# Block-sparse attention with a GELU feed-forward: the last batch's keys and queries are asked for in the middle of the fourth half's attention

## The chip, the core and the metric

The kernel runs on one core of a Trainium2 chip. The metric is the device time of one execution in microseconds (us), lower is better. The engines are PE (TensorE: matrix products), DVE (VectorE), ACT (ScalarE), POOL (GpSimd) and SP (SyncE); each works through its own list of instructions in order and waits on semaphores for the others. Transfers are asked for by an instruction on POOL or SP and are carried out by 16 DMA engines.

## What is computed

```python
# q, k, v: 4 batches x 8 heads x 768 tokens x 64, float32; blocks of 32 tokens, 24 blocks
scores = scale * np.matmul(q, k.transpose(0, 1, 3, 2))
mask = np.abs(blk_i - blk_j) <= window
mask = mask | (blk_i == 0) | (blk_j == 0) | (blk_i == n_blocks - 1) | (blk_j == n_blocks - 1)
for qb in range(n_blocks):
    for kb in sampled_blocks[qb]:                     # 3 sampled blocks per block of queries
        mask[qb*block:(qb+1)*block, kb*block:(kb+1)*block] = True
attn = softmax(np.where(mask, scores, -1e9))
x = (attn @ v), heads put side by side: 3072 tokens x 512
h = x @ w_in                                          # 512 -> 2048
out = (0.5 * h * (1 + erf(h / sqrt(2)))) @ w_out      # 2048 -> 512, float32
```

Every block of queries sees its neighbours, the first and the last block and three sampled blocks. The first and the last block of queries see everything ("dense" rounds).

## The kernel before

The 4 batches are worked in 8 **halves** (`units`), two to a batch: an even half has the quads 1, 2, 0 and the dense rounds, an odd half the quads 3, 4, 5 and sparse rounds alone. The outer loop runs over the halves n = 0 to 7. One turn of it does the first feed-forward product of half n (`ffn1_step`, 8 steps of PE products and a GELU on ACT), then the attention of half n + 1, with the second feed-forward product of half n (`ffn2_pieces`) filled in between. So the fourth half, `units[3]`, is the second half of batch 1; its attention runs in the turn n = 2, and its first feed-forward product opens the turn n = 3.

The order in an attention is written out by hand as a string of words, `PLANS[n + 1]`: `s` scores (PE), `m` maxima (DVE, into a tile `nm`), `e` exponentials (ACT, from `nm`), `t` transposes (DVE), `w` the product with the values (PE, into `av`), `d` the division (DVE, into `xh`), `o` transposes on PE and copies to `xT` (ACT), `f` some products of the second feed-forward, `S` the stores that are due (ACT copies to `os`, SP sends), `G` the table of GELU, and `x` with a name: a function handed in by the caller. An attention may end with the first two rounds of the half after the next batch's border ("ahead").

Keys and queries of a batch come in two steps. POOL asks for them by tokens into the tiles `qn` and `kn` (`load_by_token`, L126: 6 transfers of 128 KB each). Then SP turns them with a transposing transfer: `turn_queries` (L136, `qn` to `qT`) and `turn_keys` (L133, `kn` to `ptd`, in the next turn). Ahead of the loads POOL copies one element into `mark` (`hold_loads`, L172), so that nothing behind it on POOL starts before that element is written. On POOL's list the loads of a batch are followed by another such mark and by the copies of sampled blocks for the next half (`gather`, L316); DVE does most of these copies itself (L316 too), after those of the fixed blocks (L295, L308).

For the last batch (b = 3) both loads and the turning of queries are issued in the turn n = 3, after the first step of the feed-forward. There `hold_loads` takes an element of `xT` that ACT writes in the last output but one of the fourth half's attention. `nm` and `xh` are tiles of a pool with four buffers to a name, so the fifth maximum after one waits until all that read the first are done.

Of the kernel before, what the change touches and what calls it, by code (L numbers as in the profile page):

```python
# [20 lines left out]
def kernel(  # L21
# [12 lines left out]
    B, H, S, D = q.shape  # L34
# [42 lines left out]
    kn = const.tile([P, H, PI * D], BF16, name="kn")  # L77
    qn = const.tile([P, H, PI * D], BF16, name="qn")
# [22 lines left out]
    def sampled(i, r):  # L101
        c0 = GW * (i // 3) + 4 * BW + DW * (i % 3) + BW * r
        return gb[:, c0:c0 + BW]
# [9 lines left out]
    def keys(b):  # L113
        return kvs[b % 2][:, :, 0:KC]
# [5 lines left out]
    def by_token(x):  # L120
        return x.rearrange("p h c -> p (h c)")[:, 0:S * H * D // P]

    def load_by_token(dst, src, b):
        rows = by_token(dst).rearrange("p (c h d) -> p c h d", h=H, d=D)
        for c in range(NC):
            nc.gpsimd.dma_start(out=rows[:, c],  # L126
                                in_=src[b, :, P * c:P * c + P].rearrange("h p d -> p h d"))
# [7 lines left out]
    def turn_queries(b):  # L135
        nc.sync.dma_start_transpose(out=qTs[b % 2].rearrange("p c r s -> p (c r) s"), in_=by_token(qn))  # L136
# [33 lines left out]
    def hold_loads(x):  # L170

        nc.gpsimd.tensor_copy(mark, x)  # L172
# [146 lines left out]
    class Unit:  # L319
        def __init__(self, b, quads, dense):  # L320
# [10 lines left out]
            for grp in self.groups:  # L331
# [4 lines left out]
    units = [Unit(b, quads, dense) for b in range(B)  # L336
             for quads, dense in (((1, 2, 0), True), ((3, 4, 5), False))]
    groups_of = {rnd: grp for unit in units for grp in unit.ends.values() for rnd in grp}
    column = {}
    for n, unit in enumerate(units):  # L340
        for t, quad in enumerate(unit.quads):
            for i in range(4):
                column[unit.b, 4 * quad + i] = (xTs[n % 2], P * t + BL * i)

    st = {}

# [78 lines left out]
    def table(func):  # L425

        nc.scalar.activation(junk, zero[0:1, 0:1], func)  # L427
# [164 lines left out]
    def store_finished():  # L592
        while finished:
            store(*finished.pop(0))
# [17 lines left out]
    def attention(unit, filler, plan, extra={}, ahead=None):  # L612

        done = begun.pop(unit, 0)
        rounds = [(unit, rnd) for rnd in unit.rounds[done:]]
        if ahead:
            begun[ahead] = AHEAD
            rounds += [(ahead, rnd) for rnd in ahead.rounds[0:AHEAD]]  # L620
        groups = dict(zip("dabc" if unit.dense else "abc", [grp for _, grp in sorted(unit.ends.items())], strict=True))
        todo = {f"{k}{i}" for k in "smet" for i in range(len(rounds))}
        todo |= {k + c for k in "wdo" for c in groups}
        tall = False
        for word in plan.split():
            what, arg = word[0], word[1:]
            if what in "sfwoOx":

                before, tall = tall, what in "sw" and arg[0] != "d"
            if what == "s":  # L630
                at = [int(i) for i in arg.split("+")]
                scores(rounds[at[0]][0], *[rounds[i][1] for i in at])
                todo -= {f"s{i}" for i in at}
                continue
            if what == "f":
                for _ in range(int(arg)):
                    next(filler, None)
                continue
            if what == "x":
                extra[arg]()  # L640
                continue
            if what == "S":
                store_finished()
                continue
            if what == "G":
                table(AF.Gelu)
                continue
            if what in "met":
                {"m": maxima, "e": exponentials, "t": turned}[what](rounds[int(arg)][1])
            elif what == "w":  # L650
                halves = tuple(int(h) for h in arg[1:]) or (0, 1)
                values(unit, groups[arg[0]], halves, before)
                if 1 not in halves:
                    continue
                word = word[0:2]
            elif what == "d":
                divided(groups[arg])
            elif what in "oO":
                outputs(unit, groups[arg], 1 + (what == "O"))
            todo.remove(word.lower())  # L660
        assert not todo, todo
        for _ in filler:
            pass
        store_finished()
# [56 lines left out]
    def more_numbers(js):  # L721
        def load():
            for c in range(0, len(js), 6):
                known.update(block_numbers(js[c:c + 6], DVE))
        return load
# [14 lines left out]
    def next_keys(b):  # L740
# [3 lines left out]
    PLANS = {  # L744
# [20 lines left out]
    for n, unit in enumerate(units):  # L765
        nxt = units[n + 1] if n + 1 < len(units) else None
        b = unit.b
        fresh = nxt is not None and nxt.b != b
        if nxt is not None and not fresh:
            if n == 0:  # L770
                nc.vector.tensor_copy(kvs[0][:, :, 0:KC], k0)
                more_numbers(J1[3:8])()
            gather_fixed(keys(b), nxt.place)
            gather(nxt, J1[:8], known)
            if n == 0:
                more_numbers(J0[:3])()
        for s in range(KOUT // 2):
            ffn1_step(n, 2 * s)
            if s == 0:
                if n == 0:  # L780
                    hold_loads(sampled(nxt.place[J1[7]], NR - 1)[0:1, BW - 1:BW])
                    gather(nxt, J1[8:], others, engine=nc.gpsimd)
                    ones(1)
                elif fresh and b + 2 < B:
                    xT, t0 = column[b, unit.groups[-2][0]]
                    hold_loads(xT[0:1, 0, t0:t0 + 1])
                    load_by_token(qn, q, b + 2)
                    load_by_token(kn, k, b + 2)
                    turn_queries(b + 2)
                elif nxt is not None and not fresh:  # L790
                    if b + 1 < B:
                        turn_keys()
                        hold_loads(sampled(nxt.place[J1[7]], NR - 1)[0:1, BW - 1:BW])
                        load_values(b + 1)
                    else:
                        gather(nxt, J1[8:], others, engine=nc.gpsimd)
            if s == 7 and nxt is not None:
                table(AF.Exp)
                if n > 0 and not fresh and b + 1 < B:
                    next_keys(b + 1)  # L800
                    hold_loads(keys(b + 1)[0:1, NB, 0:1])
                    gather(nxt, J1[8:], others, engine=nc.gpsimd)
            if fresh and s == 0:
                gather_fixed(keys(b + 1), nxt.place)
                gather(nxt, J0[3:9], known)
                gather(nxt, J0[:3], known)
                hold_loads(sampled(nxt.place[J0[2]], NR - 1)[0:1, BW - 1:BW])
                gather(nxt, J0[9:], others, engine=nc.gpsimd)
        filler = ffn2_pieces(n)
        if nxt is None:  # L810
            last_output(n)
        elif n == 0:
            def later_values():
                hold_loads(qTs[1][0:1, 0, 1, 0:1])
                load_values(1)
            extra = {f"{w}{pr}{end}": partial(turn_pair, w, pr, end == "d")
                     for w in "kq" for pr in range(NPR) for end in ("", "d")}
            attention(nxt, filler, PLANS[1], extra | {"v": later_values, "s": partial(spare_key, keys(1))},
                      ahead=units[n + 2])
        else:  # L820
            attention(nxt, filler, PLANS[n + 1], ahead=units[n + 2] if not fresh and b + 1 < B else None)


# [28 lines left out]
```

## Time and profile before

| | |
|---|---|
| time, median of 3 runs (lowest to highest) | 273.91 us (272.92 to 274.8) |
| the profiled execution: time | 274.32 us |
| the profiled execution: span from first to last instruction | 272.5 us |
| PE, ACT, DVE, POOL busy | 93%, 76%, 75%, 38% of the span |
| packets of POOL's DMA queue (q0), of SP's (q1) | 57440 and 18418 |
| transfers from POOL for `qn` and `kn` by tokens | 12 each, 128 KB |

The profile has the time of one execution; the span leaves out what lies before the first and behind the last instruction. A page of the profile gives the busy time of each engine, then the span cut in slices, the DMA queues, the chain of work that ended last, and groups of instructions. The trace behind it can be asked for a timeline of one engine (start, length, engine, line, operation, tiles, and in brackets the idle time before it with what ended it), for the chain of waits in order of time, and for the DMA queues in a stretch of the span (packets, MB, and the time of the packets as a share of 16 engines, which passes 100% where packets overlap). In all views "issue" is time in which an engine waited for nothing that the profile shows.

### The profile page before, as it was taken

To read this page: it belongs to the slowest core of one execution; us is meant where nothing else is said; L and a number is where in the kernel's file an instruction comes from. 1 tells how busy PE (TensorE), PEld (TensorE's weight loads), DVE (VectorE), ACT (ScalarE), POOL (GpSimd) and SP (SyncE) were. 2 spreads that over 40 slices of the span, in tenths; PEclk is the share of its full clock that TensorE was granted. 3 is DMA by queue.
4 is the path that set the end of the run, shared out by engine and by line. 5 is a ranking of instruction groups with operands and counts; after the bars stand their busy time and mean duration, and the time that the engine had idled before them with its cause. 6 is when DMAs were issued, how large, how long until landed. Compare 5 with 4: busy or idle time off the path is not lost.

```text
span 272.5 us, 11555 instructions
## 1 busy us (share of the span) xinstructions
PE 252.6 (93%) x4944; PEld 144.1 (53%) x4944; DVE 203.3 (75%) x472; ACT 206.7 (76%) x381; POOL 103.6 (38%) x212
## 2 busy tenths in 40 slices
PE   0899679999999999999999799999999999999994
PEld 0634455455664656545554466455655655465543
DVE  7499659599897988699989686698869892981000
ACT  8789655977869975897779755995889956986611
POOL 7799960735964000940991002920040160000000
PEclk9999999999999999999999999999999999999999
DMA  6999399979999117921999017911101110021012
GB/s 96 186 191 149 55 147 202 206 123 143 93 172 129 43 41 158 104 28 68 98 156 172 8 41 156 117 43 44 38 1 43 43 41 0 5 79 41 0 38 82
DMA packets 75910, 24.41 MB, mean 90 GB/s; under 512 B 65489, under 2 KB 72914, under 8 KB 75858
## 3 DMA queue, kind: packets, MB, share of 16 engines
q0 software_dynamic: 57440, 13.64, 53.4%
q1 hardware_dynamic: 18418, 10.03, 15.5%
q8 instruction: 39, 0.64, 1.0%
q14 instruction: 13, 0.11, 0.1%
HBM read 27.26 MB, written 6.29 MB: 123 GB/s over the span
## 4 chain that ended last, share of the span: by engine, by line
PE 82%; ACT 7%; issue 3%; DMA 3%; DVE 3%; POOL 1%; POOLq 0%; ACTq 0%
PE hp L536 30%; PE op L579 26%; PE av L481 10%; PE sc L356 6%; DMA qn<-in_q_dram 3%; PE tx L513 2%; PE op L608 2%; ACT pp L399 2%; PE av L442 2%; PE pt L241 2%; ACT pp L403 2%; PE av L608 1%; DVE xh L501 1%; ACT L427 1%; ACT gb L295 1%
## 5 line engine op out<-in xcount | busy, mean ns | idle before, releaser
L536 PE MATMUL hp<-xT,w_in_sb 128*128 128x384 bf16 (+2 forms) x536 | 85.1, 319 | 1.4 <-issue 1.4
L579 PE MATMUL op<-w_out_sb,g 128*128 128x512 bf16 x336 | 83.4, 380 | 0.4 <-issue 0.4
L399 ACT ACTIVATE pp<-sc,nm 128x256 bf16<-128x256 f32 x176 | 74.2, 544 | 4.4 <-DVE nm L382 3.8
L536 PEld LDWEIGHTS <-w_in_sb 128*128 128x128 bf16 x536 | 51.2, 98 | 34.5 <-issue 1.5
L558 ACT ACTIVATE g<-hp 128x768 bf16<-128x768 f32 x56 | 45.1, 809 | 25.6 <-PE hp L536 25.6
L382 DVE TENSOR_REDUCE nm<-sc 128x4 f32<-128x1024 f32 (+1 forms) x48 | 53.0, 1119 | 12.3 <-PE sc L356 11.9
L579 PEld LDWEIGHTS <-g 128*128 128x128 bf16 x336 | 29.4, 98 | 33.9 <-issue 6.0
L316 DVE COPY gb<-kv 128x392 bf16 x177 | 35.8, 282 | 0.0
L416 DVE STREAM_TRANSPOSE pT<-pp 128x512 f32<-128x512 f32 (+1 forms) x48 | 30.6, 652 | 2.8 <-ACT pp L399 2.6
L172 POOL COPY mark<-gb 1x1 bf16<-1x1 bf16 x6 | 1.1, 179 | 80.9 <-DVE gb L316 80.9
L316 POOL COPY gb<-kv 128x392 bf16 x54 | 26.3, 537 | 14.1 <-PE av L481 13.8
L481 PEld LDWEIGHTS <-pT 64*32 64x32 bf16 (+1 forms) x2400 | 25.5, 91 | 7.3 <-issue 2.1
L481 PE MATMUL av<-kv,pT 64*32 64x130 bf16 (+1 forms) x1344 | 27.4, 221 | 1.7 <-issue 0.9
L521 ACT COPY xT<-tx 128x512 bf16<-128x512 bf16 (+3 forms) x34 | 13.7, 432 | 14.0 <-PE tx L513 14.0
L148 POOL DMA_DIRECT2D kv<-in_v_dram x32 | 23.0, 727 | 2.4 <-issue 2.4
L356 PE MATMUL sc<-gb,qT 64*32 64x256 bf16 x704 | 18.1, 273 | 2.2 <-issue 1.5
L356 PEld LDWEIGHTS <-qT 64*32 64x32 bf16 x832 | 9.9, 90 | 18.1 <-issue 10.0
L427 ACT ACT_TABLE_LOAD x15 | 19.2, 1283 | 0.3
L501 DVE TENSOR_TENSOR xh<-av,rec 128x512 bf16<-128x512 f32 (+2 forms) x28 | 18.2, 652 | 1.0
L385 DVE TENSOR_REDUCE nm<-sc 128x1 f32<-128x768 f32 x16 | 14.8, 949 | 4.6 <-PE sc L356 4.6
L403 ACT ACTIVATE pp<-sc,nm 128x768 bf16<-128x768 f32 x16 | 17.0, 1106 | 1.2 <-DVE nm L385 0.9
L481 PE MATMUL av<-gb,pT 64*32 64x130 bf16 x924 | 17.3, 222 | 0.5 <-issue 0.5
(80 smaller groups left out, 247.2 us busy)
## 6 DMA issues: line engine op xcount, KB each, us to landing
out_dram<-os SPq DMA_DIRECT2D x23, 256.0 KB, 2.1
kv<-in_v_dram POOLq DMA_DIRECT2D x32, 96.0 KB, 3.3
w_in_sb<-in_moe_w_in_dram POOLq DMA_DIRECT2D x4, 512.0 KB, 7.1
w_out_sb<-in_moe_w_out_dram POOLq DMA_DIRECT2D x2, 1024.0 KB, 13.5
kn<-in_k_dram POOLq DMA_DIRECT2D x4, 384.0 KB, 11.4
qn<-in_q_dram POOLq DMA_DIRECT2D x4, 384.0 KB, 12.7
qn<-in_q_dram POOLq DMA_DIRECT2D x12, 128.0 KB, 4.9
kn<-in_k_dram POOLq DMA_DIRECT2D x12, 128.0 KB, 5.3
```

The lines of the kernel that those rows point to most:

```text
L148: nc.gpsimd.dma_start(out=kvs[b % 2][32 * hh:32 * hh + 32, 0:NB, c0:c0 + D], in_=v[b, h].rearrange("(n p) d -> p n d", p=BL))
L316: (engine or nc.vector).tensor_copy(to[:, None, :], src[:, bass.ds(at[j][r], 1), :])
L356: nc.tensor.matmul(o, lhsT=qT[rows, j // 4, pr, BL * (j % 4):BL * (j % 4) + BL], rhs=rhs(rows, pr), start=True, stop=True)
L382: nc.vector.tensor_reduce(out=nm[:, 0:2 * n].rearrange("p (g j) -> p g j", g=2), in_=A4[:, :, 0:n, :], op=ALU.max, axis=AX.X, negate=True)
L399: nc.scalar.activation(at[:, x // n, x % n], A[:, a:a + 256].rearrange("p (e c k) -> p e c k", e=2, k=BL), AF.Exp, bias=nm[:, x:x + 1])
L403: nc.scalar.activation(pp[:, 0:S].rearrange("p (c k e) -> p c e k", e=2, k=BL), A[:, 0:S].rearrange("p (c e k) -> p c e k", e=2, k=BL), AF ...
L416: nc.vector.transpose(pt.rearrange("p g c x -> p (g c) x")[:, :, 64 * s:64 * (s + n)].bitcast(F32), pp[:, 0:512 * n].bitcast(F32).rearrang ...
L427: nc.scalar.activation(junk, zero[0:1, 0:1], func)
L481: nc.tensor.matmul(av[32 * s:32 * (s + w), h, VS * G:VS * G + V2], lhsT=pv[rows, G, c % 4, BL * s:BL * (s + w), c // 4], rhs=src[rows], st ...
L536: nc.tensor.matmul(hp[:, i, c0:c1], lhsT=w_in_sb[:, ki, (m + i) * P:(m + i + 1) * P], rhs=xTs[n % 2][:, ki, c0:c1], start=(ki == 0), stop= ...
L558: nc.scalar.activation(g[:, m:m + 2, 0:T], hp[:, :, 0:T], AF.Gelu)
L579: nc.tensor.matmul(op, lhsT=g[:, m, t * P:(t + 1) * P], rhs=w_out_sb[:, m, :], start=(m == 0), stop=(m == KOUT - 1))
```

## The change

The loads and the mark ahead of them become a function, `later_batch(b, x)`. For batch 2 it is called where the code stood. For batch 3 it is handed to the attention of the fourth half as the word `xl`, which stands in `PLANS[3]` behind `m2`; the mark there takes an element of the `nm` of round 2, written by that `m2`. The turning of the queries stays where it was.

```diff
+    def later_batch(b, x):
+        hold_loads(x)
+        load_by_token(qn, q, b)
+        load_by_token(kn, k, b)
...
-        3: ("f1 s3 s1 m3 s0 f5 m1 e3 f2 e1 f2 m0 t3 e0 f6 s2 m2 e2 f3 t1 f5 t0 f4 s4 m4 t2 wa s7 f1 m7 f2 e4 "
+        3: ("f1 s3 s1 m3 s0 f5 m1 e3 f2 e1 f2 m0 t3 e0 f6 s2 m2 xl e2 f3 t1 f5 t0 f4 s4 m4 t2 wa s7 f1 m7 f2 e4 "
             "f2 da f2 s5 m5 f1 t4 e7 f2 S e5 s6 m6 t5 wb S e6 oa f1 db t6 wc f1 ob dc f4 t7 oc G f1"),
...
                 elif fresh and b + 2 < B:
-                    xT, t0 = column[b, unit.groups[-2][0]]
-                    hold_loads(xT[0:1, 0, t0:t0 + 1])
-                    load_by_token(qn, q, b + 2)
-                    load_by_token(kn, k, b + 2)
+                    if b == 0:
+                        xT, t0 = column[b, unit.groups[-2][0]]
+                        later_batch(b + 2, xT[0:1, 0, t0:t0 + 1])
                     turn_queries(b + 2)
...
         else:
-            attention(nxt, filler, PLANS[n + 1], ahead=units[n + 2] if not fresh and b + 1 < B else None)
+            def batch_after():
+                later_batch(b + 2, st[nxt.rounds[2], "nm"][0:1, 0:1])
+            attention(nxt, filler, PLANS[n + 1], {"l": batch_after},
+                      ahead=units[n + 2] if not fresh and b + 1 < B else None)
```

The order of instructions is the same on every engine before and after. What differs is what POOL's mark reads, and the waits that follow from it. On POOL, around that mark (L172; `kv` and `gb` are the tiles that its copies of sampled blocks read and write; the names in brackets are the semaphores waited for: DMAHW of SP's transfers, DMASW of POOL's own):

```order
 L316 ISA
 L316 COPY gb<-kv_84 128x392 [waits PE_49]
-L172 COPY mark<-xT_92 1x1 [waits Activation_49,Pool_49]
+L172 CAST mark<-nm 1x1 [waits DVE_49,Pool_49]
 L126 DMA qn<-in_q_dram 128x8x64 [waits DMAHW2_49,DMASW2_49]
 L126 DMA qn<-in_q_dram 128x8x64 [waits DMASW3_49]
```

Only the mark's source has changed, and so the engine that releases POOL: DVE instead of ACT. On DVE, in the fourth half's attention, from the maximum that the mark now reads (`nm_3201`) to the one that takes its buffer again, before:

```order
L382 TENSOR_REDUCE nm_3201<-sc_3184 128x4 [waits PE_49]
L416 STREAM_TRANSPOSE pT_3215<-pp_3162 128x8x64 [waits Activation_49]
L416 STREAM_TRANSPOSE pT_3215<-pp_3173 128x8x64 [waits Activation_49]
L382 TENSOR_REDUCE nm_3244<-sc_3227 128x4 [waits DVE_49,PE_49]
...
L385 TENSOR_REDUCE nm_3362<-sc_3352 128x1 [waits DVE_49,PE_49]
...
L382 TENSOR_REDUCE nm_3394<-sc_3385 128x2 [waits PE_49]
...
L385 TENSOR_REDUCE nm_3415<-sc_3406 128x1 [waits PE_49]
```

and after:

```order
L387 TENSOR_REDUCE nm_3201<-sc_3184 128x4 [waits PE_49]
L421 STREAM_TRANSPOSE pT_3228<-pp_3162 128x8x64 [waits Activation_49]
L421 STREAM_TRANSPOSE pT_3228<-pp_3173 128x8x64 [waits Activation_49]
L387 TENSOR_REDUCE nm_3257<-sc_3240 128x4 [waits DVE_49,PE_49]
...
L390 TENSOR_REDUCE nm_3375<-sc_3365 128x1 [waits DVE_49,PE_49]
...
L387 TENSOR_REDUCE nm_3407<-sc_3398 128x2 [waits PE_49]
...
L390 TENSOR_REDUCE nm_3428<-sc_3419 128x1 [waits PE_49,Pool_49]
```

The last of these maxima now waits for POOL too, since POOL's mark reads the buffer that it takes.

## The prediction, made before the changed kernel was run

> **What bounds the kernel now.** I read the page first: busy times, then the chain that ended last.
>
> ```profile
> PE 252.6 (93%) x4944; PEld 144.1 (53%) x4944; DVE 203.3 (75%) x472; ACT 206.7 (76%) x381; POOL 103.6 (38%) x212
> ...
> q8 instruction: 39, 0.64, 1.0%
> ...
> PE 82%; ACT 7%; issue 3%; DMA 3%; DVE 3%; POOL 1%; POOLq 0%; ACTq 0%
> ```
>
> PE is the bound; what the other engines do matters only where it makes PE wait. The third row is a DMA queue of its own kind: 39 packets of "instruction", 0.64 MB. PE has 4944 products and 4944 weight loads, 253 instructions for each packet: I read these packets as PE's program arriving in pieces.
>
> So I went to the place that the change touches. POOL's timeline from 114 us on shows when the last batch's loads are issued now:
>
> ```profile
> 114.66 4.16 POOL L316 COPY gb<-kv 128x392 bf16 x9
> 129.36 0.30 POOL L172 COPY mark<-xT 1x1 bf16<-1x1 bf16 x1 [10.55 <-ACT xT L521]
> 129.89 6.06 POOL L126 DMA_DIRECT2D qn<-in_q_dram  x6 [0.23 <-issue]
> 135.94 5.34 POOL L126 DMA_DIRECT2D kn<-in_k_dram  x6
> ...
> 141.40 2.79 POOL L316 COPY gb<-kv 128x392 bf16 x6
> ```
>
> POOL stands idle for 10.55 us until ACT has written `xT`, then issues 12 transfers until 135.94 + 5.34 = 141.28. SP's timeline beside it:
>
> ```profile
> 121.56 10.98 SPq L565 DMA_DIRECT2D out_dram<-os  x3
> 140.29 5.48 SPq L136 DMA_TRANSPOSE qT<-qn  x1
> ```
>
> The turning of the queries starts at 140.29, when the queries have landed; the third store ahead of it is out by 121.56 + 10.98 = 132.54.
>
> Last I read the chain of waits there, for what PE lost:
>
> ```profile
> 130.55 10.40 PE hp L536 x64
> ...
> 148.65 1.25 PE av L442 x78
> 149.91 1.48 issue
> 151.38 0.47 PE av L442 x18
> ...
> 154.65 0.46 issue
> ...
> 207.49 1.49 PE av L442 x96
> ```
>
> The dense value product (L442, 96 matmuls) of the fifth half breaks off after 78 for 1.48 us with nothing to wait for. The last row is the same product of the seventh half, where no batch is loaded any more: 1.49 us in one piece. What the DMA queues did in the 4.1 us ahead of the pause, and then in the next 1.1 us:
>
> ```profile
> q1 hardware_dynamic: 1919, 0.52, 101.6%
> q0 software_dynamic: 986, 0.12, 46.9%
> ...
> q1 hardware_dynamic: 152, 0.22, 55.2%
> q8 instruction: 1, 0.02, 5.4%
> q0 software_dynamic: 8, 0.00, 1.0%
> ```
>
> From 144.8 to 148.9 us the DMA engines are full with the transposing transfer (q1) and the last keys (q0), and no piece of program comes. From 148.9 to 150.0 both run dry, one piece comes, and PE goes on at 151.38. So I take the pause for a piece of PE's program that stood behind that traffic. This is the only large loss of PE that the moved loads can touch.
>
> **The change part by part.** The order of instructions is the same on all engines; only the mark's source moves, and with it the time of the loads. DVE's timeline: copies of sampled blocks, the maximum that the mark now reads, the one that takes its buffer again, copies again, and the maximum behind them:
>
> ```profile
> 103.94 4.18 DVE L316 COPY gb<-kv 128x392 bf16 x24
> ...
> 117.53 1.23 DVE L382 TENSOR_REDUCE nm<-sc 128x4 f32<-128x1024 f32 x1
> ...
> 125.44 0.92 DVE L385 TENSOR_REDUCE nm<-sc 128x1 f32<-128x768 f32 x1
> ...
> 132.69 8.11 DVE L316 COPY gb<-kv 128x392 bf16 x27
> 141.58 1.23 DVE L382 TENSOR_REDUCE nm<-sc 128x4 f32<-128x1024 f32 x1 [0.77 <-PE sc L356]
> ```
>
> *When the loads run.* `nm` is written at 117.53 + 1.23 = 118.76, POOL's copies end at 114.66 + 4.16 = 118.82. So the mark runs at about 118.8 instead of 129.36, 10.5 us earlier, and the 12 issues fill about 119.3 to 130.5 (11.4 us before, 6.06 + 5.34). As the queries land well ahead of 132.5, SP's third store sets the turning: about 132.5 instead of 140.29. The landing times of the page:
>
> ```profile
> kn<-in_k_dram POOLq DMA_DIRECT2D x12, 128.0 KB, 5.3
> qT<-qn SPq DMA_TRANSPOSE x2, 10.8
> ptd<-kn SPq DMA_TRANSPOSE x2, 6.8
> ```
>
> The last keys land about 130.5 + 5.3 = 136, the turned queries at 132.5 + 6.8 to 10.8 = 139 to 143 (6.8 is the turning of keys, which has the queues more to itself). Both lie within PE's 10.40 us of the feed-forward, 130.55 to 140.95, or just behind it, and the queues are empty when the piece of program is due that came late at 148.9.
>
> *Gain: the pause at 149.91*, 1.48 us, goes whole: −1.48 (bounds −1.48 and 0). What hangs on that product, DVE's division and ACT's copies, moves up with it. *The pause at 154.65*, 0.46 us, comes with empty queues; it is a short block of quick products and I let it stay: 0 (bounds −0.46 and 0).
>
> *Cost: the same lateness in the fourth half's attention.* The loads now run where PE also takes program. Between 119 and 130 us, before:
>
> ```profile
> q1 hardware_dynamic: 288, 0.52, 12.8%
> q8 instruction: 2, 0.03, 1.1%
> ```
>
> Two pieces come in an almost empty DMA, and PE's chain has no issue pause there. After, q0 is full in that stretch. The nearest rows are in the second half's attention, PE's timeline, and the DMA queues from 63.4 to 65.9 us:
>
> ```profile
> 58.98 0.27 PE L481 MATMUL av<-kv,pT 64*32 64x130 bf16 x9 [0.27 <-issue]
> 67.26 1.02 PE L579 MATMUL op<-w_out_sb,g 128*128 128x512 bf16 x4 [0.36 <-issue]
> q0 software_dynamic: 2504, 0.31, 197.1%
> q8 instruction: 1, 0.02, 3.2%
> ```
>
> Here q0 was full with loads of values of the same kind (packets of about 125 bytes), and the pieces still came, with pauses of 0.27 and 0.36 us. From below the cost is 0, from above 1.48 for each of the two, the pause at 149.91. I take 0.27 + 0.36 = +0.63, since q0 alone made those, and 1.48 took the transposing transfer, which is not there then.
>
> *The mark* costs what it did (0.30 us): 0. *The new wait on DVE* stands at the maximum of 125.44; the mark is done by about 119.2, 6 us earlier: 0. Behind it on DVE stand the last transposes and divisions of that attention, for which PE's output transposes wait, so a late POOL would show; POOL's list ahead of the mark ends at 118.82, which covers it. *DVE beside POOL's issues:* its copies of sampled blocks took 8.11 / 27 = 0.30 us beside the issues and 4.18 / 24 = 0.17 us without. They would now end about 3.4 us earlier, near 137.3, and POOL's own six copies near 140 instead of 144.2. Neither is worth anything: PE's feed-forward lasts until 140.95, and DVE's next maximum already waits 0.77 us for PE. In the attention DVE now works beside the issues; what it does there:
>
> ```profile
> 61.68 0.70 DVE L416 STREAM_TRANSPOSE pT<-pp 128x512 f32<-128x512 f32 x1
> 121.71 0.70 DVE L416 STREAM_TRANSPOSE pT<-pp 128x512 f32<-128x512 f32 x1
> ```
>
> The first ran beside POOL's issues of values, the second with POOL idle, at the same 0.70: 0. *SP's queue:* stores and turning keep their order, and the three stores ahead of the turning wait for ACT alone, as before: 0.
>
> **Sum:** −1.48 + 0.63 = −0.85 us. The profiled execution took 274.32, so 273.5 against its own time; it lies 0.41 above the median, so 273.1 against the median of 273.91.
>
> **The rivals.**
> A, the forecast: the late piece comes in time and small pauses come instead; 273.91 − 1.48 − 0.46 + 0 = 272.0 at best to 273.91 − 1.48 + 1.48 = 273.9.
>
> B, nothing is gained: the pause isn't the traffic's doing but that of this place in the program, and it comes again, with or without the 0.63: 273.9 to 274.5. Against it speaks the seventh half's unbroken product, for it that one pause with one packet is a single case, and that the pause at 154.65 comes with empty queues. The Trainium skill, Runtime: NRT & Kernel Launch, section Instruction fetch mechanics, says that PE holds 2048 instructions and refills in blocks of 256, so that crossing a block is mostly hidden; by that rule a piece late by a few us would not stop PE, and the time would be B's. The trace agrees with the 256 (253 worked out above) but not with the depth: PE stopped around the very arrival of one piece.
>
> C, slower: the loads' packets hold up both pieces of program in the fourth half as the transposing transfer did at 148.9, 1.48 each: 2 × 1.48 − 1.48 = +1.48, so 275.4. It decides as soon as the two together lose more than the 1.48 gained. For it: there PE takes a piece every 3 to 4 us, not every 15 as in the feed-forward, and stores share the queues. Against it: 0.27 and 0.36 in the second half under a full q0.
>
> **How the numbers follow.** A 0.62, B 0.18, C 0.14, something else 0.06. The time is A's, 273.1. The range goes from 271.9 (both pauses gone, no new one) to 274.8 (B's upper end of 274.5, and some tenths for the spread of the runs); it holds A and B and leaves out C's upper part. About 1% (2.7 us) is what a measurement of this kernel can tell from no change: A, B and C all lie within it. For slower by over 1% C would have to double (0.05); for faster, as much would have to be found at a place that I don't see (0.03).
>
> **What would show each step.** POOL's mark at about 119 and the issues until 130.5; SP's turning near 132.5; no packet of q0 or q1 but stores after 143; the dense value product in one piece; DVE's 27 copies at some 4.7 us; in PE's waits, issue pauses of some tenths between 119 and 130. I am wrong in the gain if the pause at L442 stays though the queues are empty; in the cost if PE's issue pauses between 119 and 130 sum to over 1.5 us or to none; and altogether if DVE's maximum waits for POOL.

## The result, and the profile after

The changed kernel takes 276.85 us (median of 6 runs, 275.47 to 278.99) against 274.0 for the kernel before in the same series (272.92 to 274.8): 1.0124 times as long, 95% interval 1.0082 to 1.0167. It is slower, and the time lies above the stated range of 271.9 to 274.8. Ratios leave out executions more than 1.5% above the fastest of their kernel and medians don't, so for kernels that spread widely the two differ.

The profile after is of an execution of 277.17 us. The page, with the same lines as before:

```profile
span 275.4 us, 11555 instructions
PE 253.7 (92%) x4944; PEld 145.4 (53%) x4944; DVE 200.1 (73%) x472; ACT 206.1 (75%) x381; POOL 102.9 (37%) x212
```

The span grew by 2.9 us, PE's busy time by 1.1: PE waits more. Where, says the chain of waits around the change (start, length, what):

```profile
125.69 0.84 PE av L486 x84
126.53 0.59 issue
127.13 0.63 PE av L486 x20
...
130.73 0.14 PE tx L518
130.87 3.10 issue
133.97 0.29 PE tx L518 x3
134.25 0.86 PE op L584 x4
135.12 10.41 PE hp L541 x64
```

Two issue pauses stand in the fourth half's attention, where there was none: 0.59 and 3.10 us. The second cuts four small transposes after the first. The DMA queues from 126.3 to 131.3 us, and then to 132.5 us (packets, MB, share of 16 engines):

```profile
q0 software_dynamic: 5041, 0.64, 199.5%
q1 hardware_dynamic: 149, 0.27, 15.4%
...
q0 software_dynamic: 1391, 0.18, 230.8%
q8 instruction: 1, 0.02, 5.5%
```

In five microseconds 5041 packets of the loads pass and no piece of program; the next piece comes between 131.3 and 132.5 us, and PE goes on at 133.97. The fifth half, where the pause of 1.48 us stood before, on PE's timeline:

```profile
151.53 1.69 PE L584 MATMUL op<-w_out_sb,g 128*128 128x512 bf16 x7
153.15 1.56 PE L447 MATMUL av<-kv,ptd 64*64 64x130 bf16 x96
154.91 0.41 PE L361 MATMUL sc<-gb,qT 64*32 64x256 bf16 x16 [0.21 <-ACT pp L404]
```

The dense value product runs its 96 matmuls in one piece. So the gain came, and a larger cost of the same kind came in another place. To keep the two apart I use the length of an attention on PE, worked out from the trace: from the start of the last product of one first feed-forward to the start of the first product of the next one. Fourth half: 17.93 us before, 21.97 after, +4.04. Fifth half: 21.73 before, 20.18 after, −1.55. All other attentions behind the change agree within 0.1 us. The sum, +2.49, and 0.5 us that the profiled execution had lost ahead of the change (first feed-forward of the third half at 102.75 instead of 102.22) make the span's 2.9, with an end that is 0.2 us shorter.

POOL, SP and DVE after, each from its timeline:

```profile
119.43 0.18 POOL L172 CAST mark<-nm 1x1 bf16<-1x1 f32 x1
119.96 5.27 POOL L126 DMA_DIRECT2D qn<-in_q_dram  x6 [0.35 <-issue]
125.18 4.43 POOL L126 DMA_DIRECT2D kn<-in_k_dram  x5
129.90 0.88 POOL L126 DMA_DIRECT2D kn<-in_k_dram  x1 [0.29 <-DMA qn<-in_q_dram]
```

```profile
122.07 15.04 SPq L570 DMA_DIRECT2D out_dram<-os  x3
137.41 3.74 SPq L136 DMA_TRANSPOSE qT<-qn  x1
```

```profile
125.96 0.92 DVE L390 TENSOR_REDUCE nm<-sc 128x1 f32<-128x768 f32 x1
...
133.76 4.71 DVE L316 COPY gb<-kv 128x392 bf16 x27
```

POOL's mark and issues stand where they were forecast. DVE's maximum with the new wait has no idle time before it. The turning came at 137.41, since the third store ahead of it hangs on PE products behind the long pause (ACT copies them to `os` at 136.19).

### The profile page after: what moved, and what is told of

Read it like the earlier page. It is cut to its first block, busy times and chain, and to the rows that moved or that the text cites. A ratio compares the mean times of both kernels' runs of the same rounds, so it can differ in the third digit from the quotient of the medians.

```text
span 275.4 us, 11555 instructions
## 1 busy us (share of the span) xinstructions
PE 253.7 (92%) x4944; PEld 145.4 (53%) x4944; DVE 200.1 (73%) x472; ACT 206.1 (75%) x381; POOL 102.9 (37%) x212
## 4 chain that ended last, share of the span: by engine, by line
PE 79%; ACT 9%; issue 4%; DMA 3%; DVE 2%; POOL 1%; POOLq 0%; ACTq 0%
PE hp L541 30%; PE op L584 24%; PE av L486 10%; PE sc L361 5%; ACT pp L404 4%; DMA qn<-in_q_dram 3%; PE tx L518 2%; PE op L613 2%; ACT pp L408 2%; PE pt L241 2%; ACT L432 1%; PE av L613 1%; PE av L447 1%; DVE xh L506 1%; ACT gb L295 1%
## 5 line engine op out<-in xcount | busy, mean ns | idle before, releaser
L172 POOL COPY mark<-gb 1x1 bf16<-1x1 bf16 x6 | 1.1, 179 | 94.4 <-DVE gb L316 94.4
L316 DVE COPY gb<-kv 128x392 bf16 x177 | 32.8, 266 | 0.0
L486 PEld LDWEIGHTS <-pT 64*32 64x32 bf16 (+1 forms) x2400 | 26.7, 94 | 7.1 <-issue 1.9
L486 PE MATMUL av<-kv,pT 64*32 64x130 bf16 (+1 forms) x1344 | 28.5, 227 | 0.8 <-DVE pT L421 0.7
L486 PE MATMUL av<-gb,pT 64*32 64x130 bf16 x924 | 17.5, 223 | 0.7 <-issue 0.6
```

The costliest lines, as they stand in the source:

```text
L316: (engine or nc.vector).tensor_copy(to[:, None, :], src[:, bass.ds(at[j][r], 1), :])
L486: nc.tensor.matmul(av[32 * s:32 * (s + w), h, VS * G:VS * G + V2], lhsT=pv[rows, G, c % 4, BL * s:BL * (s + w), c // 4], rhs=src[rows], st ...
```

## The experiments

Theory T: PE's program comes in pieces over the same DMA engines, and a piece that is asked for while many packets of the loads are queued comes late; PE stands until it is there. The rivals are named in the expectations; their letters are not those of the prediction. The table has, from each profile, the two issue pauses in the fourth half's attention and the lengths of the fourth and the fifth half's.

| kernel | median us | ratio to before, 95% | pauses, us | fourth | fifth |
|---|---|---|---|---|---|
| before | 274.0 | | none | 17.93 | 21.73 |
| before, second profile (e11) | 274.17 | 1.0005 (0.9971 to 1.0038) | none | 17.93 | 20.97 |
| changed | 276.85 | 1.0124 (1.0082 to 1.0167) | 0.59, 3.10 | 21.97 | 20.18 |
| changed, second profile (e6) | 277.81 | 1.0177 (1.0115 to 1.024) | 1.41, 3.37 | 23.07 | 19.62 |
| e1: mark alone, no loads | 273.26 | 0.9957 (0.9925 to 0.9989) | none | 17.93 | 19.62 |
| e2: queries alone early | 274.83 | 1.0039 (1.001 to 1.0068) | none, 0.90 | 19.31 | 19.61 |
| e2, second profile (e12) | 274.61 | 1.0013 (0.9982 to 1.0043) | 1.97, none | 20.33 | 19.62 |
| e3: behind m5 | 273.01 | 0.9968 (0.9947 to 0.9989) | none | 17.93 | 19.62 |
| e4: behind m6 | 272.63 | 0.9957 (0.9935 to 0.9979) | none | 17.93 | 19.64 |
| e4 again (e10) | 272.92 | 0.9974 (0.9943 to 1.0006) | none | 18.14 | 19.65 |
| e5: loads early and late | 277.06 | 1.0103 (1.0061 to 1.0145) | 1.71, 2.82 | 23.08 | 19.62 |
| e7: two in flight | 277.19 | 1.0044 (1.0001 to 1.0086) | 0.61, 0.35 | 19.24 | 22.44 |
| e8: two stores less | 276.19 | 1.0103 (1.0071 to 1.0136) | 0.86, 0.62 | 19.76 | 19.62 |
| e9: three in flight | 273.59 | 0.9987 (0.9959 to 1.0015) | 0.58, 0.63 | 19.49 | 20.14 |

**e1, the mark without the loads.** In the function handed to the attention:

```diff
-                later_batch(b + 2, st[nxt.rounds[2], "nm"][0:1, 0:1])
+                hold_loads(st[nxt.rounds[2], "nm"][0:1, 0:1])
```

> The changed kernel with the mark on nm kept and the 12 loads of the last batch left out (the last batch then works on the queries and keys of batch 2, so its output differs). Theory T (pieces of PE's program stand behind the packets of the loads): both issue pauses of PE in the fourth half (0.59 and 3.10 us) go, and the pause of 1.48 us in the dense value product of the fifth half too: 274.0 - 1.5 = 272.5 us (272.0 to 273.2). Rival M (the mark on nm, the new wait on DVE and the new order of releases cost the time, the transfers are innocent): 276 us or more, with DVE or POOL as releaser in PE's waits.

Both pauses went, the fourth half is back at 17.93 and the fifth at 19.62; the median fell by 0.6 us, to 273.26 (against 273.84 in that series), a little less than T gave (273.2 at most). The mark and its waits are innocent: rival M falls. It shows the gain too, 2.1 us between the profiles: without any late packets the dense product and what follows it run through.

**e2, the queries alone early, and e12, the same once more.**

```diff
+                    xT, t0 = column[b, unit.groups[-2][0]]
                     if b == 0:
-                        xT, t0 = column[b, unit.groups[-2][0]]
                         later_batch(b + 2, xT[0:1, 0, t0:t0 + 1])
+                    else:
+                        hold_loads(xT[0:1, 0, t0:t0 + 1])
+                        load_by_token(kn, k, b + 2)
...
-                later_batch(b + 2, st[nxt.rounds[2], "nm"][0:1, 0:1])
+                hold_loads(st[nxt.rounds[2], "nm"][0:1, 0:1])
+                load_by_token(qn, q, b + 2)
```

> The changed kernel, but only the queries' 6 loads are issued behind m2; the keys' 6 stay where they were before, behind the mark on xT. T: the queries' packets run dry near 128 us, so the second piece comes in time and the pause of 3.10 us goes, the first of 0.59 stays, and the pause at the dense value product stays away, since the queries are turned early: 274.0 - 1.5 + 0.6 = 273.1 us (272.5 to 274.0). Rival A (any loads of this kind in that attention hold PE up, however many): 276 to 277 us.

> The kernel with the queries' loads behind m2 and the keys' at the old place, once more, for a second profile: its median was 1.0 us above the kernel before, though in its profile the fourth half's attention lost 1.4 us and the fifth's gained 2.1. V: the two pauses in the fourth half sum to another value than 1.0 us, up to 3; F: 0.9 to 1.2 us again.

Half the loads cost 1.4 us of the fourth half's attention in the one profile and 2.4 in the other, instead of 4.0 to 5.2; the long second pause shrank to 0.90 and to none. The median lies above T's range and below A's. So the amount matters, against A, but six loads are not free, and the pauses differ from execution to execution, as V had it.

**e3 and e4, all loads, but later in the same attention.** The word `xl` leaves its place behind `m2` (in the string's first line, not shown) for a later one, and the mark reads the `nm` of that round:

```diff
# e3
-            "f2 da f2 s5 m5 f1 t4 e7 f2 S e5 s6 m6 t5 wb S e6 oa f1 db t6 wc f1 ob dc f4 t7 oc G f1"),
+            "f2 da f2 s5 m5 xl f1 t4 e7 f2 S e5 s6 m6 t5 wb S e6 oa f1 db t6 wc f1 ob dc f4 t7 oc G f1"),
# e4
+            "f2 da f2 s5 m5 f1 t4 e7 f2 S e5 s6 m6 xl t5 wb S e6 oa f1 db t6 wc f1 ob dc f4 t7 oc G f1"),
```

> All 12 loads in the fourth half's attention, but behind m5 (near 124.9 us) instead of m2 (118.8). T: their packets start near 127, when the piece that came at 131.4 in the changed kernel has been asked for and is nearly in; no pause over 0.5 us in the fourth half, and none at the dense value product, since the queries land near 135 and are turned by about 144: 272.8 us (272.2 to 274.0). Rival A (loads anywhere in that attention cost about 3 us): 276 us or more.

> As behind m5, but behind m6 (near 126.4 us), 3 us before the place that the kernel before has. T: no pause in the fourth half, since no packet of the loads runs before 128; the turning ends near 145, so the pause at the dense value product is gone or below 0.7 us: 272.6 us (272.2 to 273.6). Rival A: 276 us or more; a rival L (it is the time of the turning alone that sets the pause at the dense product, and 3 us are too little): 273.5 to 274.2 us.

Neither has a pause in the fourth half, and both have the whole gain in the fifth. PE's timeline of e4 there:

```profile
146.89 1.68 PE L584 MATMUL op<-w_out_sb,g 128*128 128x512 bf16 x7
148.51 1.55 PE L447 MATMUL av<-kv,ptd 64*64 64x130 bf16 x96
150.28 0.41 PE L361 MATMUL sc<-gb,qT 64*32 64x256 bf16 x16 [0.22 <-DVE den L501]
```

and its POOL:

```profile
126.42 0.18 POOL L172 CAST mark<-nm 1x1 bf16<-1x1 f32 x1 [7.57 <-DVE nm L390]
126.95 6.26 POOL L126 DMA_DIRECT2D qn<-in_q_dram  x6 [0.35 <-issue]
133.19 5.35 POOL L126 DMA_DIRECT2D kn<-in_k_dram  x6
```

The same 12 loads, the same mark and the same kind of wait, 7 us later than in the changed kernel and 3 us earlier than in the kernel before: now the last piece of program that the attention needs has been sent (its packet runs from 126.82 to 127.81) before the first packet of the loads at 128.57, and the turning is done before a piece is next due in the fifth half. A and L fall.

**e10, e4 once more.**

> The loads behind m6 once more, on another chip or at another time, to see whether the gain stands: T says 0.4% under the kernel before, 272.2 to 273.2 us; if the first result was an accident of that chip, as rival C has it, the interval of the ratio holds 1.0.

The median is 1.05 us below the kernel before in that series (273.97) and in T's range, but the interval reaches to 1.0006. The gain, 0.43% in e4 and 0.26% here, was clear of 1.0 once, so by the sign that the expectation names an accident is not ruled out; e3's 0.32%, clear of 1.0 too, speaks against one. The profile shows the same as e4's.

**e5, the loads both early and late.**

```diff
-                    if b == 0:
-                        xT, t0 = column[b, unit.groups[-2][0]]
-                        later_batch(b + 2, xT[0:1, 0, t0:t0 + 1])
+                    xT, t0 = column[b, unit.groups[-2][0]]
+                    later_batch(b + 2, xT[0:1, 0, t0:t0 + 1])
```

> The changed kernel, with the same 12 loads issued once more at the old place (behind the mark on xT), so that the cost of the loads in the fourth half's attention stands without the gain. T (pieces of PE's program stand behind the loads' packets): both pauses in the fourth half stay (some 3.7 us together), and with the late packets back a part of the pause at the dense value product may come again: 277 to 279 us. Rival G (the time comes from what else moved earlier, the turning and the copies of sampled blocks, not from packets in the attention): 274 to 275 us.

277.06 us, with 1.71 and 2.82 us of pauses; the cost comes from early packets, and G falls. The late packets brought no pause back in the fifth half, where PE by then was some 5 us later. This profile, of the longest of the four executions (279.01 us), has another loss: the feed-forward behind the pauses took 11.78 us on PE in the chain instead of 10.41, at a granted clock of 0.88 from 136 to 148 us; it was 1.00 around that feed-forward in the changed kernel.

**e6, the changed kernel once more.**

> The changed kernel once more, on the same chip as the others, for its spread and for the two pauses in a second profile. T: 276 to 278 us, two issue pauses of PE between 119 and 135 us, together 2.5 to 4.5 us. If the pause of 3.10 us was one execution's accident, as rival X has it, they sum to less than 1.5 us.

On PE's timeline:

```profile
126.73 0.29 PE L486 MATMUL av<-gb,pT 64*32 64x130 bf16 x12 [1.41 <-issue]
...
133.84 0.29 PE L518 MATMUL tx<-identity,xh 96*128 96x96 bf16 x3 [3.37 <-issue]
```

The same two places, 4.78 us together, over what I had expected. X falls: it was no accident.

**e7 and e9, not more than two and three loads in flight.** The 12 loads in a row, each (from the third or fourth on) behind a mark on an older one:

```diff
-                later_batch(b + 2, st[nxt.rounds[2], "nm"][0:1, 0:1])
+                hold_loads(st[nxt.rounds[2], "nm"][0:1, 0:1])
...
+                for i, (dst, src, c) in enumerate(loads):
+                    if i >= 2:                                    # e9: 3
+                        hold_loads(tiles[i - 2][0:1, 0, 0:1])     # e9: i - 3
+                    nc.gpsimd.dma_start(out=tiles[i],
+                                        in_=src[b + 2, :, P * c:P * c + P].rearrange("h p d -> p h d"))
```

> The changed kernel, but ahead of each load from the third on POOL reads an element of the load before the last, so that never more than two of the 12 loads are in flight. The same packets run through the same attention, spread over more time. TB (a piece waits behind the packets that are queued when it is asked for, so the backlog of issued loads sets the pause): at most two loads of some 1.1 us of full queues each stand ahead of a piece; the pause of 3.10 us falls below 0.7 and the two together to 1 us or less: 272.5 to 273.8 us. TS (a piece is slowed by any running traffic of that queue, backlog or not): the pauses stay at 2.5 us or more together: 275.5 us or more.

> As with two loads in flight (where the pauses of PE in the fourth half shrank, but POOL's copies of sampled blocks came at 150 us and PE waited for them in the fifth), now with up to three: the loads end earlier and the copies should be done by 146. TB (the backlog of issued loads sets the pause): the two pauses sum to 1 to 2 us, between those of two in flight (1.0) and of all twelve (3.7 to 4.8); 274 to 275 us, and the fourth half's attention takes 19 to 20 us against 17.9 before. TS (any running traffic does it): 2.5 us or more, 276 us.

With two in flight the pauses sum to 0.96 us and the fourth half takes 19.24, but the time didn't follow: 277.19 us, far above TB's range and where TS had put it. The ten executions spread from 274.11 to 280.44 us, and the profile is of one of 279.01. In it 2.5 us are lost ahead of the change (the third half's feed-forward starts at 104.69 instead of 102.22), before any of the moved loads is issued, and POOL was held so long that its copies of sampled blocks came late, so that PE waited for them in the fifth half. On PE's timeline:

```profile
152.05 0.30 PE L361 MATMUL sc<-gb,qT 64*32 64x256 bf16 x8 [1.44 <-POOL gb L316]
153.42 0.30 PE L361 MATMUL sc<-gb,qT 64*32 64x256 bf16 x8 [1.06 <-POOL gb L316]
```

With three, that wait is gone and the pauses are 0.58 and 0.63; 273.59 us, a little below the range and no different from before. The pauses fell from between 3.7 and 4.8 to 1.2, while packets of the same kind still ran: TS, in which any running traffic is enough, falls. TB alone is not shown by it. The limit also thins the traffic: between 119 and 131 us 6240 packets of the loads pass instead of 7989 in the changed kernel, as many as in e2 (6235), whose pauses lie on both sides of e9's. Whether the loads queued at once or the packets that run set the length stays open.

**e8, without the two stores in that stretch.** In `store`:

```diff
-        nc.sync.dma_start(out=out[row:row + P, cols], in_=os)
+        if n != 2 or quad == units[n].quads[-1]:
+            nc.sync.dma_start(out=out[row:row + P, cols], in_=os)
```

> The changed kernel without the two stores of the third half that run in the fourth half's attention (their rows of the output are not written). TB: the stores take some 1.5 us of the queues each, so the loads' backlog is shorter by that and the pause of 3.10 us falls to 1 to 2: 274.5 to 276 us. Rival S (the pieces stand behind the stores, and the loads matter only as they delay these): both pauses go, 272.5 us.

In the profile the pauses shrink to 1.48 together, but they don't go, and the median is 276.19, just above TB's range: the loads alone are enough, against S. By the profile alone I would have expected less time than that; one profile is one draw of the pauses, and this one is of an execution of 275.05 us, 1.1 below the median. How much the stores add to the pauses is not shown.

**e11, the kernel before once more.**

> The kernel before once more, for a second profile. The measured gains of the kernels whose loads run late in that attention (1.2 and 1.1 us) are smaller than the 2.1 us by which the fifth half's attention shortened between the profiles (21.7 to 19.6). V (the pauses differ from execution to execution, and the first profile of the kernel before shows a long one): here the fifth half's attention takes 20 to 21.3 us, with a first pause below 1.2 us. F (the pauses are fixed, the gain is lost elsewhere): 21.5 us or more, with pauses of 1.5 and 0.5 us as in the first profile.

Its chain of waits:

```profile
148.97 1.25 PE av L442 x78
150.22 0.45 issue
150.67 0.47 PE av L442 x18
...
153.93 0.74 issue
```

The same two places with 0.45 and 0.74 instead of 1.48 and 0.46, and the fifth half takes 20.97 us: V holds. The change was worth 1.35 us (20.97 to 19.62) to 2.1 us there; the first profile showed a large draw.

## Why the prediction was wrong

*When the loads run* was right: the mark at 119.43 (forecast 118.8), the last issue ending at 130.78 (130.5). The turning came at 137.41 instead of 132.5, as a result of the long pause.

*The gain* was right in its mechanism and near in size: −1.48 forecast, −1.55 in the profile, and −1.35 to −2.1 in the profiles of the kernels without any early cost, by which of the two profiles of the kernel before one takes; their medians fell by less, 0.6 to 1.2 us. "The pause at 154.65 … I let it stay" was too careful: in e4 PE's `av` products of that place (L486) run in one piece.

*The costs put at nothing* were nothing: the mark, DVE's new wait, and DVE beside POOL's issues. DVE's 27 copies took 4.71 us, as forecast (4.7), hidden behind PE's feed-forward.

The step that failed is the term "*Cost: the same lateness in the fourth half's attention*", put at 0.27 + 0.36 = +0.63 us "since q0 alone made those, and 1.48 took the transposing transfer". It measured +4.04 and +5.14 in the two profiles. The reason given was wrong: the transposing transfer is not needed, q0, with 149 packets of the stores beside it, made a pause of 3.10. The price was wrong too. Of the two pauses in the second half that I took for it, the one of 0.27 us ended at 58.98, before POOL issued the first of those loads:

```profile
59.02 5.64 POOL L148 DMA_DIRECT2D kv<-in_v_dram  x8
```

Only 0.36 was measured under a full q0. There q0 was just as busy (197% against 199.5%), but with less queued behind it. The busy share can't show that (in e8 it is 181% between 119 and 131 us, against 131.7% in the changed kernel, and the pauses are less than half as long); the time from issue to landing shows more. The issues of the stretch from 63.4 to 65.9 us before, and of that from 119 to 131 us after (KB each, median us to landing):

```profile
kv<-in_v_dram POOLq DMA_DIRECT2D x2, 96.0 KB, 4.3
```

```profile
qn<-in_q_dram POOLq DMA_DIRECT2D x6, 128.0 KB, 6.6
kn<-in_k_dram POOLq DMA_DIRECT2D x6, 128.0 KB, 7.2
```

In the profiles with all 12 loads in a row the pauses go with that time: landing in 6.6 to 7.2 us comes with 3.7 to 4.8 us of pauses, e8's 5.8 and 5.9 with 1.48. With three and with two in flight it is 5.0 and 4.1 for the queries' loads, with pauses of 1.21 and 0.96. The queries alone don't fit in: they landed in 6.9 and 6.6 us in e2's two profiles, with pauses of 0.90 and 1.97.

What the prediction also missed is that PE had no time to spare there. The two places lie 127 products and 128 weight loads apart, one piece (253 instructions on average). In the kernel before, the piece for the second place had come in at 128.05, and PE passed there at 129.39, 1.34 us later, without a pause; where PE does pause in these profiles for want of a piece, it goes on 1.3 to 1.7 us after the piece's end. So in the changed kernel a piece that began 4.36 us later (131.36 instead of 127.00) cost nearly all of it, 4.04.

My bound from above, 1.48 for each piece, was the longest pause that I had found, which is no bound: both second pauses of the changed kernel passed it twice over. *Rival C* was this mechanism, and its condition, two pauses of more than 1.48 us together, came true; it had 275.4 us and a chance of 0.14; the time of 276.85 lies above that too. *Rival B*, and with it the rule of the Trainium skill (Runtime: NRT & Kernel Launch, section Instruction fetch mechanics) that crossing a block of PE's program is mostly hidden, doesn't hold at these two places: PE stood there in both profiles of the changed kernel, and at neither in e1, e3 and e4. Most of the 39 pieces do come without a pause.

What stays open: why a piece has to wait for so many packets of another queue; and how long the pauses are over many executions, since each run shows them in one profile alone. For e2 and e8 the median is 1 to 3 us above what the pauses in their first profile would give; 1.1 us of that, in each, is that the profiled execution was a quick one (273.74 and 275.05). That the spread of the pauses makes up the rest was argued from e11, e12 and e6, and not shown; e5's clock and e7's late start show that other things spread as well.

## What to carry to other kernels

An issue pause of PE in a stretch of short products is worth a look at the instruction packets in the DMA queues: if none comes while a data queue is full and the pause ends 1.3 to 1.7 us after one has come, the loads are holding up the program. Loads then go where PE needs no new program for long, here the feed-forward, and the last place ahead of it is behind the last piece that the attention needs: 3 us earlier than before took 0.43% in one series and 0.26% in the other, the second not clear of no change, and 10 us earlier cost 1.2%. How busy the queue is doesn't give the price; the time from issue to landing was the better sign here. And a place without a pause is not yet a place with time to spare: read how long before it its piece of program had come.

## What the runs showed of the hardware

A piece of 16 KB on a queue of its own came late while packets of another queue passed. After the first pause of the changed kernel PE went on at 127.13, and the next piece began at 131.36, 4.23 us later, with 4303 packets of the loads in between. In the kernel before, with 8 packets of data in the queues from 150 to 152.4 us, PE went on at 151.38 and the next piece began 1.05 us later. The Trainium skill, DMA: Bandwidth & Descriptors, section Queues, rings and completion order, says that each DMA engine takes turns between its queues packet by packet; by that rule I would expect a piece that is asked for to come within a few packets. The trace doesn't show when it is asked for; it shows the 4303 packets, and what keeps the piece back was not tried.

DVE's copies of sampled blocks took 0.30 us each beside POOL's issues of loads (8.11 / 27, before) and 0.17 us without (4.71 / 27, after). What slows them is not shown.
